# A planner's rules and costs in a causal convolution with a top-2 mixture of experts: idle slots filled, GpSimd and waits costed anew, row scatters spread further, margin of filled rows 2.2 instead of 3.0

## The chip, the cores and the metric

The kernel runs on one core of one Trainium2 chip. The time is in device microseconds for one execution; lower is better. Engines are named as in the profile: PE (matmul), PEld (weight load), DVE (vector), ACT (scalar), POOL (GpSimd) and SP (sync, here an issuer of DMAs).

## The reference

```python
# 1. causal depthwise convolution, 7 taps, softmax weights per head (8 heads of 24 columns)
w = softmax(weight, axis=-1)                       # 8 x 7
out[b, s, h, :] = sum_k w[h, k] * x_pad[b, s + k, h, :]
x = out.reshape(28672, 192)
# 2. top-2 of 8 experts, 192 -> 1024 -> 192
noisy = x @ w_gate + log1p(exp(x @ w_noise)) * noise
top2  = indices of the two largest of noisy;  g = softmax over those two
for e in range(8):
    y[rows of e] += g[rows of e] * (relu(x[rows of e] @ w1[e]) @ w2[e])
```

## The kernel before, in words

**Tiling.** The 28,672 tokens are worked in 28 units of 1,024 (`U`, `TU` = 8 tokens on each of 128 partitions). A unit is loaded (`xt`), convolved (PE for the first three units, then DVE lines L560 and L562), scaled, split into two fp16 parts (`rb`, two buffers), and its gate logits are formed on PE (L637). DVE then runs the routing chain (L658 to L702), PE counts ranks (L709 for units 0 to 4, L721 and L723 later, fed by `sums` of L719), DVE turns ranks into row numbers (L726 to L747), and POOL scatters the unit's rows to the region of each expert in DRAM: 16 indirect DMAs of 128 rows of 800 bytes each (L768), two for each of the 8 tokens of a partition.

**Blocks.** An expert's region is read in rounds, the first of 128 rows, then 28 of 256. A block is one round of one expert, 232 in all. SP loads it transposed (`bT`, L908 and L911, three buffers), PE runs 40 matmuls into `ph` (L848, two halves of 20), ACT and DVE evacuate each half into `h` as a high and a low part (L854, L858), PE runs 24 matmuls for each 128 rows into `py` (L866), ACT scales them into `y` (L872, six buffers) and POOL adds the rows to the output in DRAM with one indirect DMA for each 128 rows (L877). PE interleaves: the first product of block n, then the second of block n-1. At the start each expert's weights are split as well: `gram` on PE (L364), ACT the high part (L410), DVE the low part (L412).

**What sets the order.** Each engine executes its instructions in the order in which the program emits them. That order comes from a list scheduler in the kernel's own text: `Plan` keeps a clock for each engine and a set of threads (`conv`, `gating`, `scatters`, `run_blocks`, `results` and so on). A thread yields `(engine, cost)` before each piece, or a point in planned time, or a mark that another thread sets. `Plan.run` emits the piece with the smallest start minus urgency. No clock of the plan is in the built program: a cost there only moves an instruction to another place in its engine's order. Only semaphores hold an instruction back on the chip.

**Scatters and their pacing.** `scatters(u)` yields POOL 16 times with a pause of up to 2.0 planned us behind each, less when the unit's due time is near. Between two of them the plan may emit additions (L877).

**Rows that a round may read.** `ready_unit` says after how many units a round's rows are taken to be full: mean count less 3.0 sigma. A round's loads wait on the scatters of the units up to that one, and `lmin` pushes a later unit's rows behind any round already open to reading. An expert with more than 7,296 rows would run extra blocks in a loop at the end. For these inputs the eight experts get 7,067 to 7,242 rows; no unit is pushed by `lmin`, with 3.0 or with 2.2, and no extra block runs.

Of the kernel before, what the change touches and what calls it, by code (L numbers as in the profile page):

```python
# [19 lines left out]
TU = 8  # L20
# [25 lines left out]
class Plan:  # L46
# [5 lines left out]


    GAP = 0.1

    def __init__(self, **clock):
        self.clock, self.threads, self.now = clock, [], 0.0
# [32 lines left out]
    def run(self):  # L90
        self.spawned = []
        while True:
            best = None
            for th in self.threads:
                if th[1] is None:
                    continue
                eng = th[1][0]
                at = max(self.clock[eng], th[0] + (self.GAP if th[4] != eng else 0.0))
                if len(th[1]) > 2:
                    free = th[1][2].ready()  # L100
                    if free is None:
                        continue
                    at = max(at, free)
                urge = th[3](at) if callable(th[3]) else th[3]
                if best is None or at - urge < best[0]:
                    best = at - urge, at, th
            if best is None:
                assert not self.threads, "threads wait for each other"
                return
            _, at, th = best  # L110
            op = th[1]
            if len(op) > 2:
                op[2].taken += 1
            self.now = th[0] = self.clock[op[0]] = at + op[1]
            th[4] = op[0]
            self.step(th)
            while self.spawned:
                self.step(self.spawned.pop())
# [6 lines left out]
def kernel(  # L125
# [25 lines left out]
    mean = P * TU * 2 // E  # L151
# [4 lines left out]

    def ready_unit(end):
        for u in range(U):
            if mean * (u + 1) - 3.0 * sigma * math.sqrt(u + 1) >= end:
                return u  # L160
        return U - 1

# [100 lines left out]
    def done(*key, after=0.0):  # L263
        plan.mark(mark(*key), after)
# [329 lines left out]
    def gating():  # L594
        for u in range(U):
# [9 lines left out]
            if u < NTR:  # L605
                for t in range(0, 3 * TU, 8):
                    yield PE, 0.6, py_ring
                    if xT is None:
                        xT = small.tile([P, TU, 3, P], F16, name="xT", bufs=1)
                    pt = psum.tile([P, 512], F32, name="py", bufs=2)  # L610
                    pt = pt.bitcast(F16).rearrange("p (t n) -> p t n", n=P)
                    for i in range(8):
                        nc.tensor.transpose(pt[:, i], rb[:, (t + i) // 3, (t + i) % 3 * P:((t + i) % 3 + 1) * P], ident16)  # L613
                    yield ACT, 1.05
                    nc.scalar.activation(xT.rearrange("p t c n -> p (t c) n")[:, t:t + 8, :], pt, AF.Copy)
                    plan.freed(py_ring)
            else:
                for t in range(TU):
                    yield SP, 1.27
                    if xT is None:  # L620
                        xT = small.tile([P, TU, 3, P], F16, name="xT", bufs=1)
                    nc.sync.dma_start(xT[:, t], rb[:, t, 0:384], transpose=True)  # L622
                yield plan.now + 2.5
            if u == 0:
                yield mark("gates")
            yield PE, 1.1 if u < NTR else 0.7
# [80 lines left out]
            if u < NTR:  # L707
                yield PE, 0.45
                nc.tensor.matmul(rk[:, :TU * E], before, M.rearrange("p t e -> p (t e)"), start=True, stop=False,  # L709
                                 skip_group_check=True)  # L710
                for t in range(TU):
                    nc.tensor.matmul(rk[:, (t + 1) * E:W], ones16,
                                     M[:, t, None, :].to_broadcast([P, TU - t, E]),
                                     start=False, stop=(t == TU - 1), skip_group_check=True)
            else:
                yield DVE, 0.7
                sums = small.tile([P, TU + 1, E], F16, name="sums")
                with nc.allow_low_precision("counts of at most eight"):
                    V.tensor_reduce(sums, windows(Ms[u % 2]), axis=AX.X, op=OP.add)  # L719
                yield PE, 0.1  # L720
                nc.tensor.matmul(rk[:, :W], ones16, sums.rearrange("p t e -> p (t e)"), start=True, stop=False,  # L721
                                 skip_group_check=True)
                nc.tensor.matmul(rk[:, :TU * E], before, M.rearrange("p t e -> p (t e)"), start=False, stop=True,  # L723
                                 skip_group_check=True)
# [34 lines left out]
    def scatters(u, rbf, idx):  # L759
        if u:  # L760
            yield mark("scattered", u - 1)
        if reach[u + 1] > lo_row:
            yield mark("zero rows")
        for i in range(2 * TU):
            t, k = i // 2, i % 2
            yield POOL, 1.05
            apart()
            s = nc.gpsimd.indirect_dma_start(  # L768
                out=xsf, out_offset=bass.IndirectOffsetOnAxis(ap=idx[:, k, t:t + 1], axis=0),
                in_=rbf[:, t, :], in_offset=None)  # L770
            for v in scat:
                tc.declare_no_dep(s.ins, group=f"scat{v}", reason="every routed row has its own place")
            tc.declare_no_dep(s.ins, group="loads", reason="rows behind those of the blocks done")
            scat[u].append(s)
            tc.add_to_no_dep_group(f"scat{u}", s.ins)
            if reach[u + 1] > lo_row:
                for z in init:
                    needs(s, z)
            slack = (due(u) - 40.0 - plan.now) / (2 * TU - i)
            if u > 1:  # L780
                yield plan.now + min(2.0, max(0.0, slack - 1.0))
        done("scattered", u, after=2.5)

    def load_meta(j):
# [129 lines left out]
            done("block", n, after=2.3)  # L914

    def round_meta(j, mt):
        yield plan.now + 2.3
        if j:
            yield mark("first", (j - 1) * E + E - 3)
            yield mark("scale", E - 1)  # L920
        yield DVE, 1.9
        s, T = rounds[j]
        metas[j] = meta(mt, T // P, runs[:, ready[j] + 1, :], float(s))
        if j:
            unscale(metas[j][1], slice(0, E), T // P)
        done("meta", j)
        if j == 0:
            for e in range(E):
                yield mark("scale", e)
                yield DVE, 0.2  # L930
                unscale(metas[0][1][:, e:e + 1, :], slice(e, e + 1), T // P)
                done("gate", e)
# [9 lines left out]
    def results(n, half, py, adds):  # L942
# [7 lines left out]
        plan.freed(py_ring)  # L950
        if n:
            yield mark("added", n - 1)
        yield POOL, 1.6
        add_rows(j, ids[:, e, half:half + 1], y, adds)
        plan.freed(y_ring, 2.0)
        if half == rounds[j][1] // P - 1:
            done("added", n, after=2.5)

    def second(n):
        j, e = blocks[n]  # L960
# [105 lines left out]
```

## Time and profile before

| | |
|---|---|
| median of 3 runs | 2117.39 us (2103.3, 2117.39, 2119.4) |
| the profiled execution | 2097.99 us, its span 2096.2 us |
| busy share of the span | PE 95%, PEld 85%, DVE 75%, POOL 61%, ACT 38% |
| blocks | 232, 9,280 first and 10,944 second matmuls |

The page gives busy time by engine, the span in 40 slices, the DMA queues, the chain that ended last and the costliest groups of instructions. Behind it stand views of the trace: busy time in chosen stretches, waits (who waited for whom), and the instructions of an engine in order of time. "issue" in a wait means that the engine waited for nothing that the profile shows.

### The profile page before, as it was taken

To read this page: it belongs to the slowest core of one execution; us is meant where nothing else is said; L and a number is where in the kernel's file an instruction comes from. 1 tells how busy PE (TensorE), PEld (TensorE's weight loads), DVE (VectorE), ACT (ScalarE), POOL (GpSimd) and SP (SyncE) were. 2 spreads that over 40 slices of the span, in tenths; PEclk is the share of its full clock that TensorE was granted. 3 is DMA by queue.
4 is the path that set the end of the run, shared out by engine and by line. 5 is a ranking of instruction groups with operands and counts; after the bars stand their busy time and mean duration, and the time that the engine had idled before them with its cause. 6 is when DMAs were issued, how large, how long until landed. Compare 5 with 4: busy or idle time off the path is not lost.

```text
span 2096.2 us, 52494 instructions
## 1 busy us (share of the span) xinstructions
PE 1983.7 (95%) x21703; PEld 1778.0 (85%) x21703; DVE 1565.0 (75%) x4042; ACT 803.3 (38%) x1173; POOL 1271.8 (61%) x915
## 2 busy tenths in 40 slices
PE   7557999999999999999999999999999999999997
PEld 6546888878888899889899998988898888999986
DVE  6677888878888898889988888889899753333232
ACT  4334343333334343443343434433443433333332
POOL 0353576765666776777667777777767665333333
PEclk9778999999999999999999999999999999999999
DMA  8733456876657677666777766677777664444442
GB/s 238 196 91 79 86 98 118 155 148 118 117 92 125 130 132 128 122 126 117 118 129 133 126 130 117 113 120 131 130 132 115 107 98 77 58 61 57 60 58 35
DMA packets 521882, 236.99 MB, mean 113 GB/s; under 512 B 401304, under 2 KB 508824, under 8 KB 521505
## 3 DMA queue, kind: packets, MB, share of 16 engines
q1 hardware_dynamic: 433824, 142.72, 33.2%
q0 software_dynamic: 87200, 90.80, 29.3%
q8 instruction: 171, 2.80, 0.6%
q14 instruction: 79, 0.65, 0.1%
q10 hardware_dynamic: 608, 0.02, 0.0%
HBM read 40.12 MB, written 115.38 MB: 74 GB/s over the span
## 4 chain that ended last, share of the span: by engine, by line
PE 88%; DVE 5%; issue 3%; SPq 2%; ACT 1%; DMA 1%; another core or an unknown queue 0%; ACTq 0%; POOL 0%; DVEq 0%; POOLq 0%
PE ph L848 43%; PE py L866 41%; PE ph L514 1%; SPq L622 1%; PE misc L637 1%; DVE h L858 1%; PE grams L364 1%; DVE xc L562 0%; DMA xT<-rb 0%; DVE w1s L412 0%; SPq L911 0%; DVE w2s L412 0%; PE py L613 0%; DVE t L673 0%
## 5 line engine op out<-in xcount | busy, mean ns | idle before, releaser
L877 POOL DMA_INDIRECT out_dram<-y,ids x456 | 776.0, 1702 | 593.2 <-ACT y L872 423.5
L848 PE MATMUL ph<-bT,w1s 128*128 128x256 f16 (+2 forms) x9280 | 1004.7, 273 | 26.6 <-issue 10.3
L866 PE MATMUL py<-w2s,h 128*128 128x192 f16 x10944 | 953.1, 246 | 12.0 <-issue 11.3
L848 PEld LDWEIGHTS <-w1s 128*128 128x128 f16 (+1 forms) x9280 | 773.2, 98 | 210.6 <-issue 116.6
L866 PEld LDWEIGHTS <-h 128*128 128x128 f16 x10944 | 910.0, 98 | 23.8 <-issue 18.3
L858 DVE SCALAR_TENSOR_TENSOR h<-ph,h 128x1024 f16<-128x1024 f32 (+1 forms) x464 | 557.5, 1203 | 389.8 <-ACT h L854 345.2
L854 ACT ACTIVATE h<-ph 128x1024 f16<-128x1024 f32 (+1 forms) x464 | 468.0, 1009 | 556.8 <-PE ph L848 469.1
L768 POOL DMA_INDIRECT xs<-rb,idx x448 | 494.2, 1103 | 212.7 <-issue 144.7
L562 DVE SCALAR_TENSOR_TENSOR xc<-xt,wt,xc 128x192 f32<-128x192 f32 x1224 | 422.9, 410 | 3.3 <-DMA xt<-zero 3.3
L872 ACT ACTIVATE y<-py,ga 128x192 f32<-128x192 f32 x456 | 191.5, 421 | 602.2 <-PE py L866 439.2
L514 PE MATMUL ph<-xt,dg 128*128 128x192 f32 x280 | 50.8, 339 | 14.9 <-DMA xt<-in_x_dram 11.6
L514 PEld LDWEIGHTS ph<-xt,dg 128*128 128x128 f32 x280 | 47.3, 197 | 15.3 <-DVE dg L494 11.5
L560 DVE TENSOR_SCALAR xc<-xt,wt 128x192 f32<-128x192 f32 x204 | 53.9, 330 | 1.2 <-DMA xt<-in_x_dram 0.5
L575 DVE TENSOR_REDUCE am<-xc 128x8 f32<-128x1536 f32 x28 | 49.0, 1752 | 4.4 <-ACT xc L569 3.7
L579 DVE TENSOR_TENSOR xc<-xc,xs 128x1536 f32<-128x1536 f32 x28 | 49.3, 1761 | 0.0
L637 PE MATMUL misc<-gparts,xT 128*128 128x32 f16 (+1 forms) x752 | 27.4, 175 | 16.7 <-issue 15.3
L673 DVE SCALAR_TENSOR_TENSOR t<-t,t 128x64 f32<-128x64 f32 x168 | 38.1, 227 | 5.7
L637 PEld LDWEIGHTS <-xT 128*128 128x128 f16 x752 | 24.4, 97 | 19.8 <-issue 17.6
L589 DVE TENSOR_TENSOR rb<-xc,rb 128x1024 f16<-128x1024 f32 x28 | 34.1, 1217 | 4.3 <-ACT rb L585 2.1
L585 ACT ACTIVATE rb<-xc 128x1024 f16<-128x1024 f32 x28 | 29.5, 1053 | 11.1 <-DVE xc L579 9.3
L483 ACT ACTIVATE xt<-xt 128x1152 f32<-128x1152 f32 x27 | 31.2, 1156 | 0.0
L719 DVE TENSOR_REDUCE sums<-M 128x72 f16<-128x576 f16 x23 | 27.0, 1172 | 0.0
(142 smaller groups left out, 620.0 us busy)
## 6 DMA issues: line engine op xcount, KB each, us to landing
out_dram<-zero SPq DMA_DIRECT2D x28, 768.0 KB
xt<-in_x_dram SPq DMA_DIRECT2D x27, 768.0 KB
bT<-xs SPq DMA_TRANSPOSE x464
out_dram<-y,ids POOLq DMA_INDIRECT x456
xs<-rb,idx POOLq DMA_INDIRECT x448
w2s<-in_moe_w_dram SPq DMA_DIRECT2D x16, 384.0 KB
w1s<-in_moe_w_dram SPq DMA_DIRECT2D x8, 512.0 KB
w1s<-in_moe_w_dram SPq DMA_DIRECT2D x16, 256.0 KB
```

What stands on the lines that cost most here:

```text
L514: nc.tensor.matmul(c[:, h - h0, :TU * G].rearrange("p (t g) -> p t g", g=G), diag[h, k], xts[u][:, k:k + TU, h * G:(h + 1) * G], start=(k ...
L560: V.tensor_scalar(dst, src, wt[:, h, k:k + 1], None, op0=OP.mult)
L562: V.scalar_tensor_tensor(dst, src, wt[:, h, k:k + 1], dst, op0=OP.mult, op1=OP.add)
L579: V.tensor_tensor(xc, xc, xsc[:, :, None].to_broadcast([P, TU, D]), op=OP.mult)
L637: nc.tensor.matmul(lg[:, t], xT[:, t, c, :], g[:, gc], start=(i == 0), stop=(i == len(seq) - 1))
L768: s = nc.gpsimd.indirect_dma_start(out=xsf, out_offset=bass.IndirectOffsetOnAxis(ap=idx[:, k, t:t + 1], axis=0), in_=rbf[:, t, :], in_offs ...
L848: nc.tensor.matmul(ph[:, f, :T], w, x, start=f // 2 not in banks[:i], stop=f // 2 not in banks[i + 1:], skip_group_check=True)
L854: nc.scalar.activation(h[:, 0, half * nf:(half + 1) * nf, :T], ph[:, :, :T], AF.Relu)
L858: V.scalar_tensor_tensor(h[:, 1, hs, :T], ph[:, :, :T], 0.0, h[:, 0, hs, :T], op0=OP.max, op1=OP.subtract)
L866: nc.tensor.matmul(py[:, :D], h[:, a, f, ts], w2_part(e, lo, f), start=(n == 0), stop=(n == 3 * FC - 1))
L872: nc.scalar.activation(y, py[:, :D], AF.Copy, scale=gate)
L877: a = nc.gpsimd.indirect_dma_start(out=out, out_offset=bass.IndirectOffsetOnAxis(ap=ids, axis=0), in_=y, in_offset=None, compute_op=OP.add)
```

## The change

Six edits, all in the planner's rules and in the costs that threads yield:

- `Plan.run` collects every thread that could go (`able`). When the chosen piece would start late, another piece for the same engine that would end before that start goes first.
- A piece that follows one on PE in the same thread starts 0.3 later in the plan (`DRAIN`).
- Planned costs: a scatter 1.4 (was 1.05), an addition 2.0 (1.6), `sums` 1.1 (0.7) and 1.0 more before its matmul, the transposed rows of the logits 5.0 (2.5), a round's row data 4.0 (2.3), an added block 2.8 behind (2.5).
- The pause behind a scatter goes up to 2.6 (was 2.0).
- `ready_unit` takes 2.2 sigma (3.0). Rounds 9 to 16 then count as full one unit earlier; all others stand as before.

```diff
+    DRAIN = 0.3
...
-            best = None
+            best, able = None, []
...
-                at = max(self.clock[eng], th[0] + (self.GAP if th[4] != eng else 0.0))
+                gap = 0.0 if th[4] == eng else self.GAP + (self.DRAIN if th[4] == "PE" else 0.0)
+                at = max(self.clock[eng], th[0] + gap)
...
+                able.append((at - urge, at, th))
                 if best is None or at - urge < best[0]:
-                    best = at - urge, at, th
+                    best = able[-1]
...
+            for one in able:
+                if one[2][1][0] == best[2][1][0] and one[1] + one[2][1][1] <= best[1]:
+                    if one[0] < best[0] or one[1] < best[1]:
+                        best = one
...
-            if mean * (u + 1) - 3.0 * sigma * math.sqrt(u + 1) >= end:
+            if mean * (u + 1) - 2.2 * sigma * math.sqrt(u + 1) >= end:
...
-                yield plan.now + 2.5
+                yield plan.now + 5.0
...
-                yield DVE, 0.7
+                yield DVE, 1.1
...
+                yield plan.now + 1.0
                 yield PE, 0.1
...
-            yield POOL, 1.05
+            yield POOL, 1.4
...
-            slack = (due(u) - 40.0 - plan.now) / (2 * TU - i)
+            slack = (due(u) - 45.0 - plan.now) / (2 * TU - i)
             if u > 1:
-                yield plan.now + min(2.0, max(0.0, slack - 1.0))
+                yield plan.now + min(2.6, max(0.0, slack - 1.4))
...
-        yield plan.now + 2.3
+        yield plan.now + 4.0
...
-        yield POOL, 1.6
+        yield POOL, 2.0
...
-            done("added", n, after=2.5)
+            done("added", n, after=2.8)
```

No instruction is added or removed on PE, DVE, ACT or SP; the order moves. Line numbers of the changed kernel are 7 or 8 higher from the margin on (L768 becomes L776, L877 becomes L885, L858 becomes L866).

**POOL, unit 6.** The order on POOL around the scatters (L768) of unit 6, with the additions (L877, two for a block of 256 rows) between them. Before:

```order
L768 DMA xs<-rb_190,idx 287744x200 x5
L877 DMA out_dram<-y,ids 28928x192 x2
L768 DMA xs<-rb_190,idx 287744x200 x5
L877 DMA out_dram<-y,ids 28928x192 x2
L768 DMA xs<-rb_190,idx 287744x200 x4
L877 DMA out_dram<-y,ids 28928x192 x2
L768 DMA xs<-rb_190,idx 287744x200 x2
```

And now:

```order
L776 DMA xs<-rb_190,idx 287744x200 x2
L885 DMA out_dram<-y,ids 28928x192 x2
L776 DMA xs<-rb_190,idx 287744x200 x3
L885 DMA out_dram<-y,ids 28928x192 x2
L776 DMA xs<-rb_190,idx 287744x200 x3
L885 DMA out_dram<-y,ids 28928x192 x2
L776 DMA xs<-rb_190,idx 287744x200 x3
L885 DMA out_dram<-y,ids 28928x192 x2
L776 DMA xs<-rb_190,idx 287744x200 x2
L885 DMA out_dram<-y,ids 28928x192
L776 DMA xs<-rb_190,idx 287744x200
L885 DMA out_dram<-y,ids 28928x192
```

Five scatters to a block became three, and the last two (not shown) stand behind the tenth addition. Additions between the first and the last scatter of a unit, before and now: unit 2: 1, 2; unit 3: 7, 8; units 4 to 8: 6 each, now 10, 8, 10, 10, 8; unit 9: 8, 8; unit 10: 9, 8; unit 11: 10, 11; unit 12: 10, 12; units 13 to 27: 12 to 13, now 12 to 14.

**DVE, behind the routing of unit 1.** `h` are the low parts of the first blocks, `w1s` and `w2s` low parts of weights, `rb` the rows of unit 2. Before:

```order
L579 TENSOR_TENSOR xc<-xc,xs 128x1536
L858 SCALAR_TENSOR_TENSOR h<-ph,h 128x4x128 x2
L412 SCALAR_TENSOR_TENSOR w1s_131<-w1s_132,ws,w1s_131 128x1024
L589 TENSOR_TENSOR rb_190<-xc,rb_190 128x8x128
L591 TENSOR_TENSOR rb_190<-xc,rb_190 128x8x64
L858 SCALAR_TENSOR_TENSOR h<-ph,h 128x4x128 x2
```

And now, where behind `w1s_131` (which follows `xc`) ten small instructions of the first round's row data come first:

```order
L824 TENSOR_TENSOR ga<-ga,mt 128x8
L825 TENSOR_TENSOR ga<-ga,gb 128x8
L596 TENSOR_TENSOR rb_190<-xc,rb_190 128x8x128
L598 TENSOR_TENSOR rb_190<-xc,rb_190 128x8x64
L866 SCALAR_TENSOR_TENSOR h<-ph,h 128x4x128 x2
```

The first block's low parts moved behind a weight split, ten small instructions and the two of `rb`.

**ACT, from the first blocks to unit 2's routing.** `t` is the exponential inside unit 2's routing chain, `h` the high parts, `xT` the transposed rows for unit 2's logits. Before:

```order
L615 ACTIVATE xT<-py 128x1024 x2
L872 ACTIVATE y<-py,ga 128x192
L615 ACTIVATE xT<-py 128x1024
L483 ACTIVATE xt<-xt 128x1152
L854 ACTIVATE h<-ph 128x4x128
L662 ACTIVATE t_1419<-t_1419 128x64
L854 ACTIVATE h<-ph 128x4x128
L872 ACTIVATE y<-py,ga 128x192
L704 ACTIVATE d<-d 128x8
```

And now:

```order
L622 ACTIVATE xT<-py 128x1024
L490 ACTIVATE xt<-xt 128x1152
L622 ACTIVATE xT<-py 128x1024
L862 ACTIVATE h<-ph 128x4x128
L622 ACTIVATE xT<-py 128x1024
L862 ACTIVATE h<-ph 128x4x128
L417 ACTIVATE w1s_132<-w1s_133,ws 128x1024
L417 ACTIVATE w2s_149<-w2s_150,ws 128x768
L669 ACTIVATE t_1486<-t_1486 128x64
```

On PE, likewise, the first product of block 2 now stands ahead of unit 2's logits and not between logits and ranks, and the weight split of the expert after it moved ahead of the exponential.

## Rows read from the trace of the kernel before

**Rows 1.** The page: the span, and the instruction queue (packets, MB, share).

```profile
span 2096.2 us, 52494 instructions
...
q8 instruction: 171, 2.80, 0.6%
```

**Rows 2.** Busy time by stretch: us, then per engine busy (xinstructions), PEclk, DMA share, GB/s.

```profile
97.00:200.00 103.00, 65.11 (x729) 55.98 (x727) 76.62 (x221) 39.05 (x53) 46.29 (x39) 0.75 0.30 70
200.00:2083.00 1883.00, 1856.35 (x20467) 1662.78 (x20465) 1426.55 (x3602) 725.08 (x1048) 1204.37 (x848) 1.00 0.64 110
```

**Rows 3.** Waits of PE over the span: us in total, times, longest us.

```profile
PE misc L709 <- DVE M L702: 17.3, 2, 11.7
PE misc L637 <- issue: 15.3, 22, 1.2
...
PE py L866 <- issue: 11.3, 25, 1.2
PE ph L848 <- issue: 10.3, 25, 1.2
PE ph L848 <- DVE w1s L412: 7.4, 4, 3.3
...
PE grams L364 <- issue: 5.7, 8, 1.1
...
PE misc L721 <- DVE sums L719: 2.2, 3, 1.3
```

**Rows 4.** Busy time from first to last scatter of units 4 to 11 and 14.

```profile
298.50:333.10 34.60, 31.70 (x321) 27.48 (x319) 26.78 (x61) 12.27 (x17) 28.16 (x22) 0.96 0.69 139
369.90:407.60 37.70, 36.03 (x402) 31.94 (x401) 32.09 (x74) 15.22 (x21) 30.61 (x22) 1.00 0.82 155
433.40:467.80 34.40, 30.21 (x286) 24.38 (x284) 26.21 (x65) 10.73 (x15) 27.99 (x22) 0.90 0.78 158
496.20:535.10 38.90, 36.01 (x383) 31.86 (x381) 32.29 (x73) 15.20 (x21) 30.69 (x22) 1.00 0.73 150
560.50:594.40 33.90, 30.55 (x303) 26.11 (x302) 26.06 (x55) 11.28 (x16) 27.50 (x22) 0.95 0.76 165
622.00:663.60 41.60, 41.07 (x463) 36.79 (x461) 37.73 (x82) 17.04 (x26) 32.97 (x24) 1.00 0.76 149
683.80:726.50 42.70, 41.25 (x455) 35.94 (x452) 35.97 (x83) 15.35 (x23) 32.90 (x25) 1.00 0.72 146
743.10:791.20 48.10, 48.10 (x544) 43.51 (x542) 43.96 (x109) 20.07 (x29) 38.23 (x26) 1.00 0.76 139
...
924.40:976.90 52.50, 52.45 (x592) 47.63 (x590) 47.38 (x118) 21.73 (x33) 38.90 (x28) 1.00 0.70 131
```

**Rows 5.** POOL in time: start, us, what [idle before <-releaser]; units 6, 14.

```profile
444.99 1.07 POOL L768 DMA_INDIRECT xs<-rb,idx  x1 [0.30 <-issue]
...
928.11 1.74 POOL L877 DMA_INDIRECT out_dram<-y,ids  x1 [1.47 <-ACT y L872]
```

**Rows 6.** SP in time: zeros written to the output in units 6 and 11.

```profile
442.43 0.58 SPq L433 DMA_DIRECT2D out_dram<-zero  x1
...
763.28 0.43 SPq L433 DMA_DIRECT2D out_dram<-zero  x1
```

**Rows 7.** DVE in time, behind the routing of unit 1 and in that of unit 2.

```profile
103.34 1.28 DVE L412 SCALAR_TENSOR_TENSOR w1s<-w1s,ws,w1s 128x1024 f16<-128x1024 f32 x1
...
106.28 1.28 DVE L858 SCALAR_TENSOR_TENSOR h<-ph,h 128x512 f16<-128x512 f32 x2
...
130.12 0.16 DVE L389 TENSOR_SCALAR wf<-misc 128x4 int32<-128x4 int32 x1 [0.99 <-PE misc L247]
...
132.90 0.69 DVE L858 SCALAR_TENSOR_TENSOR h<-ph,h 128x512 f16<-128x512 f32 x1 [0.93 <-ACT h L854]
...
143.35 1.28 DVE L412 SCALAR_TENSOR_TENSOR w1s<-w1s,ws,w1s 128x1024 f16<-128x1024 f32 x1
```

**Rows 8.** PE in time: half of block 2's first product.

```profile
127.37 2.20 PE L848 MATMUL ph<-bT,w1s 128*128 128x128 f16 x20
```

## The prediction, made before the changed kernel was run

> **What bounds the kernel.** I read the page first, then busy time by stretch, then PE's waits, then the same two views again around the scatters of single units, and last the engines in order of time. The span is 2096.2 us [rows 1]. From 200 to 2083 us PE is busy for 1856.4 of 1883.0 us at the full clock [rows 2]; every microsecond that PE loses there moves the end, and nothing else does. From 97 to 200 us PE is busy for only 65.1 of 103 us, at a mean granted clock of 0.75 (a mix of the levels 1.2 and 2.4 GHz), while DVE is busy for 76.6 [rows 2]. So there are two places to gain: that opening, and the 27 us idle later on.
>
> The reader should then look at what ended PE's idle time [rows 3]. The four rows with "issue" sum to 15.3 + 11.3 + 10.3 + 5.7 = 42.6 us: PE stood still although no tile, no semaphore and no buffer was late. They are many short gaps of up to 1.2 us (80 in all). What the wait is for is my reading, not a row: instructions reach the engines by DMA, 171 packets of together 2.80 MB on a queue of their own [rows 1], so a matmul can be late because its instruction is.
>
> **When it happens** is in [rows 4], one row for each unit from its first scatter to its last. Undisturbed PE starts 592 matmuls in 52.5 us (unit 14) or 544 in 48.1 (unit 11), 11.3 a microsecond. By that rate units 4 to 8 should have done their matmuls in 28.4, 35.6, 25.3, 33.9 and 26.8 us; they took 34.6, 37.7, 34.4, 38.9 and 33.9. The loss is 6.2 + 2.1 + 9.1 + 5.0 + 7.1 = 29.5 us, slow matmuls at the lower clock included (the clock column reads 0.90 in unit 6). Unit 9, in 41.6 us, lost 0.6; unit 10, in 42.7, lost 2.4; units 11 and 14 nothing. The difference is how close the 16 scatters stand. In units 4 to 8 there are six additions between first and last scatter, five scatters to a block. A scatter takes about 1.07 us behind a gap of 0.30, an addition 1.74 [rows 5], so five and two cost 5 x 1.37 + 2 x 2.04 = 10.9 us on POOL against 8.1 us for a block (88 matmuls and its share of 26 for a unit's logits and ranks, 91 at 11.3 a microsecond): POOL issues without pause, [0.30 <-issue]. In unit 14 it waits for `y`, and so runs at PE's pace [rows 5].
>
> **The change, part by part.**
>
> *Scatters of units 3 to 11.* Three scatters and two additions cost 3 x 1.37 + 2 x 2.04 = 8.2 us, about a block. Units 4, 6 and 7 get ten additions between first and last, as unit 11 had: loss 0 by that row. Units 5 and 8 get eight, as unit 9 had: 0.6 each. Unit 10 goes from nine to eight. The upper bound of the gain is therefore 29.5 - 1.2 = 28.3, say 29 us; the lower is 0, if spacing has nothing to do with it. Unit 10, with more additions than unit 9, lost more, so the count does not settle it alone. I charge each of units 4 to 8 with unit 10's 2.4 us: 29.5 - 12 = 17.5, taken as **18 us gained**.
>
> *Unit 2.* Its scatters stood as nine, one addition, seven; now five, one, five, one, six. PE's starvation in that stretch is the larger part of the 5.7 us on L364 [rows 3] and a little on L866. I take 3 us gained, bounds 0 and 5.7.
>
> *The first blocks.* `h` of the first block ran 2.9 us behind the weight split that followed it closely before (103.34 to 106.28 is that split and the two of `rb` [rows 7]); now these and ten small instructions at 0.16 us or a little more, about 1.3 us, come first: block 1 starts 4.2 us later. Block 2's first product moves ahead of the logits: 2 x 2.20 = 4.4 us [rows 8]. Against that, unit 2's chain loses the waits of 0.99 and 0.93 and two low parts of 0.69 [rows 7], and gains one split of 1.28: 1.9 + 1.4 - 1.3 = 2.0 us shorter, with three tiny rows besides. PE stood idle for 17.3 - 11.7 = 5.6 us for this chain [rows 3]. If instructions arrive no faster than before up to the logits, PE does the moved work while it would have starved, and the ranks come about 2 us earlier; if not, up to 3 us later (4.2 + 4.4 less the 5.6 idle before). I take 0. Behind the ranks, block 3 waited for a split that began only at 143.35 [rows 7], with 3.3 us as the longest such wait [rows 3]; that split now stands inside the chain. I take 3 us gained, bounds 0 and 5. The opening together: 0 + 3 + 3, **6 us gained**, bounds 11 gained and 6 lost (3 for the ranks, 3 more if the longer idle time drops the clock as it did around the waits of this stretch, mean 0.75 [rows 2]).
>
> *Later waits for logits and ranks.* The added 2.5 and 1.0 in the plan move PE's instructions behind more blocks. L721's 2.2 us [rows 3] go: **2 us gained**, bounds 2 gained and 1 lost.
>
> *The rest is free.* The margin moves the loads of rounds 9 to 16 to one unit less; PE shows no wait on a block load in [rows 3], so there is nothing to shorten, and no unit is pushed in either version. Later scatters in units 13 to 27 end some blocks later but stay ahead of their round. An x load now issued one block sooner stands in SP's queue ahead of a block's load; three buffers hide that, and it would cost only if SP waited longer than a block.
>
> **Sum.** 18 + 6 + 2 = 26 us against the profiled 2097.99: 2072. That execution was below all three timed ones; their median is 19.4 us higher. I subtract from the median: 2117.4 - 26 = **2091 us**.
>
> A rule speaks against this. The Trainium skill, Runtime: NRT & Kernel Launch, section Instruction fetch mechanics, says that instructions are streamed in 16 KiB blocks during execution and that the cost of crossing one is "mostly hidden". The trace agrees on the size (2.80 MB in 171 packets) and not on the cover: 42.6 us of issue gaps. By the rule spacing would give nothing, and the time would be that of the first rival.
>
> **The rivals.**
>
> 1. *Not the spacing.* The starved stretches also hold the zero write of 768 KB and the x load. In unit 6 the zero write was issued at 442.43 [rows 6], within its window. If such transfers starve PE, whatever the scatters do, only 6 + 2 us are left: 2109. For: each dense window holds one. Against: the zero write of unit 11's stretch was issued at 763.28 [rows 6], within 743.1 to 791.2, and cost nothing [rows 4].
> 2. *The opening loses.* The low parts come 4.2 us late, the clock stays down and the ranks slip: 6 lost, while the spacing gives half, 9. With 2 for the later waits: 2117 + 6 - 9 - 2 = 2112.
> 3. *Slower.* Units 13 to 27 now scatter over up to 14 additions of the 16 of a round. If the pause between two units' scatters is what lets instructions catch up, its shrinking starves every unit. At unit 10's 2.4 us, 16 units from 12 to 27 lose 38 us: 2117 + 38 - 8 = 2147. It decides once units from 13 on show issue gaps of 1 us each or more. Against it: wider has always meant less in [rows 4].
> 4. *The plan does not reach the chip.* POOL's pace is set by `y` and by its own instructions, not by the plan's clock, and bunches of three may starve PE as well as five do. Then 2117.
>
> **How the numbers follow.** My forecast gets 0.55, rival 1 0.20, rival 2 0.10, rival 3 0.08, rival 4 0.07. The bounds are 2117 - 29 - 11 - 2 = 2075 and, from the profiled execution's level 19 us lower, some way below that; the upper side takes in rivals 1, 2 and 4. Range **2066 to 2119**; it leaves out rival 3 and the ends of the others. Within 1% (21 us) a measurement of this kernel can't tell a change from none: the four executions shown here differ by that much. Faster by over 1% is below 2096. The forecast at 2091 is only 5 us beyond, with bounds wide on both sides: 0.8 of its 0.55, and little of rivals 1 and 2, make 0.49. Slower takes rival 3, 0.08. The rest, 0.43, is within 1%.
>
> **What would show it.** In the profile after: windows from first to last scatter of units 4 to 8 over 40 us wide with 11 matmuls a microsecond; the four issue rows of PE at 25 us or less in sum, nearly all of it before 170 us; PE busy for over 1850 us between 200 us and its last matmul, with that matmul 20 us or more sooner; the ranks of unit 2 at their old time, give or take 3 us, and the first block of 256 rows some 6 us sooner. Wrong would be: wide windows with the same gaps (rivals 1, 4), gaps in units 13 and later (rival 3), or a wait of PE for `h` or a block load that was not there.

## The result, and the profile after

| | before | after |
|---|---|---|
| first comparison, 4 runs each | 2114.63 us median (2103.3 to 2119.4) | 2089.97 us median (2087.42 to 2096.86) |
| ratio | | 0.9896, interval 0.9849 to 0.9944 |
| last comparison, 14 and 7 runs | 2097.11 us median | 2082.01 us median, ratio 0.991 (0.9876 to 0.9944) |
| a comparison on another chip, 28 and 12 runs | 2040.71 us median | 2045.3 us median, ratio 1.0013 (0.998 to 1.0046) |

The change saves about 1%: 24.7 us by the medians of the first comparison, 15.1 by the larger last one. On another chip, where the kernel before is 74 us faster, it saves nothing. Below, the chip of the last comparison is called A (its profiles look like those of the first) and the other B.

The two profiled executions of the first comparison differ by less than the medians, 2097.99 and 2087.42 us: that of the kernel before was faster than all four timed ones. Of these 10.6 us, 6.4 are won before PE's first block of 256 rows (it started at 198.45, now at 192.09), the rest behind it.

**Span and stretches.** From the page, then busy time by stretch (columns as in [rows 2]), profile after:

```profile
span 2085.6 us, 52483 instructions
...
q8 instruction: 171, 2.80, 0.6%
```

```profile
97.00:200.00 103.00, 69.56 (x785) 59.55 (x783) 84.29 (x241) 43.48 (x59) 47.74 (x40) 0.76 0.34 81
200.00:2073.00 1873.00, 1848.23 (x20403) 1655.12 (x20400) 1412.79 (x3580) 718.83 (x1043) 1198.94 (x847) 1.00 0.65 110
```

PE is busy 4.5 us more in the opening than in [rows 2]. Behind it, 26.6 us of idle time became 24.8: hardly less.

**Waits of PE** after, the same view as [rows 3]:

```profile
PE ph L856 <- issue: 17.9, 41, 1.0
PE misc L716 <- DVE M L709: 15.8, 2, 9.5
PE misc L644 <- issue: 11.8, 14, 1.9
...
PE py L874 <- issue: 8.0, 22, 1.1
PE ph L856 <- ACT w1s L417: 6.6, 3, 4.9
PE ph L856 <- DVE h L866: 6.5, 2, 6.2
```

The issue rows sum to 37.7 us against 42.6. The 2.2 us on `sums` are gone. The wait of 6.2 us for `h` (1.6 before) is for the low parts of the first block, which the change put behind ten small instructions.

The issue rows again, behind 200 us alone, before and after:

```profile
PE ph L848 <- issue: 10.3, 25, 1.2
PE py L866 <- issue: 9.7, 23, 1.2
PE misc L637 <- issue: 1.0, 3, 0.6
```

```profile
PE ph L856 <- issue: 12.9, 30, 1.0
PE py L874 <- issue: 7.3, 20, 1.1
PE misc L644 <- issue: 1.4, 3, 0.5
```

They sum to 21.0 us before and 21.6 after. Behind the opening the starvation (PE's idle time that the profile puts down to "issue") did not become less in this profile; it moved.

**Around the scatters** after, busy time from first to last scatter of units 4, 5, 6, 7, 8, 9, 10, 11 and 14, the view of [rows 4]:

```profile
291.30:341.90 50.60, 49.84 (x556) 44.66 (x555) 44.10 (x106) 19.80 (x29) 41.01 (x26) 1.00 0.76 133
368.10:420.50 52.40, 49.44 (x538) 42.69 (x535) 43.37 (x122) 16.02 (x26) 29.30 (x24) 1.00 0.84 170
432.40:475.90 43.50, 42.29 (x469) 37.41 (x467) 37.16 (x108) 14.66 (x23) 34.00 (x26) 1.00 0.86 130
486.90:531.30 44.40, 43.09 (x482) 38.29 (x479) 38.71 (x99) 16.11 (x24) 36.77 (x26) 1.00 0.70 129
549.30:595.70 46.40, 45.60 (x513) 41.10 (x511) 42.05 (x112) 17.79 (x26) 37.50 (x24) 1.00 0.68 118
615.80:653.70 37.90, 35.34 (x389) 30.72 (x387) 29.90 (x72) 11.70 (x18) 30.86 (x24) 1.00 0.76 136
682.40:724.70 42.30, 39.20 (x409) 32.98 (x407) 33.62 (x90) 13.41 (x21) 32.89 (x24) 0.96 0.61 104
736.50:785.40 48.90, 46.34 (x512) 40.81 (x510) 42.11 (x105) 18.01 (x26) 37.45 (x27) 1.00 0.67 117
917.30:978.30 61.00, 61.00 (x685) 55.23 (x683) 55.52 (x144) 25.46 (x37) 42.58 (x30) 1.00 0.71 125
```

By 11.3 matmuls a microsecond, units 4 to 8 now lose 1.4, 4.8, 2.0, 1.7 and 1.0, together 10.9 us; in [rows 4] they lost 29.5. That is 18.6 us won. But units 9, 10 and 11 lose 3.5, 6.1 and 3.6, where they lost 0.6, 2.4 and nothing: 10.2 us given back. Unit 9's window became narrower (37.9 from 41.6 us), unit 10's stayed as it was (42.3 from 42.7), unit 11's too (48.9 from 48.1). Unit 12, not shown, loses 2.4 more than before. Unit 14 loses 0.4.

These counts differ between executions of one order. In `after_third`, the changed kernel once more, units 4 to 8 lose 11.9 us and units 9 to 11 lose 3.4, 2.6 and 2.5.

### The profile page after: what moved, and what is told of

Same layout as the page of the kernel before. It is cut to its first block, busy times and chain, and to the rows that moved or that the text cites. A ratio compares the mean times of both kernels' runs of the same rounds, so it can differ in the third digit from the quotient of the medians.

```text
span 2085.6 us, 52483 instructions
## 1 busy us (share of the span) xinstructions
PE 1980.8 (95%) x21703; PEld 1774.8 (85%) x21703; DVE 1559.3 (75%) x4042; ACT 801.1 (38%) x1173; POOL 1267.9 (61%) x915
## 4 chain that ended last, share of the span: by engine, by line
PE 91%; DVE 3%; issue 2%; another core or an unknown queue 1%; SPq 1%; ACT 1%; DMA 0%; ACTq 0%; POOL 0%; DVEq 0%; POOLq 0%
PE ph L856 45%; PE py L874 42%; PE ph L521 2%; PE misc L644 1%; SPq L629 1%; PE grams L371 0%; DVE xc L569 0%; DVE h L866 0%; DVE w1s L419 0%; PE py L620 0%; DVE xc L567 0%; ACT h L862 0%; DMA xt<-zero 0%; DVE dg L501 0%
## 5 line engine op out<-in xcount | busy, mean ns | idle before, releaser
L885 POOL DMA_INDIRECT out_dram<-y,ids x456 | 798.5, 1751 | 572.5 <-ACT y L880 415.7
L866 DVE SCALAR_TENSOR_TENSOR h<-ph,h 128x1024 f16<-128x1024 f32 (+1 forms) x464 | 557.9, 1203 | 339.3 <-ACT h L862 307.0
L776 POOL DMA_INDIRECT xs<-rb,idx x448 | 467.8, 1044 | 226.5 <-issue 138.1
L644 PE MATMUL misc<-gparts,xT 128*128 128x32 f16 (+1 forms) x752 | 26.0, 175 | 12.9 <-issue 11.8
L592 ACT ACTIVATE rb<-xc 128x1024 f16<-128x1024 f32 x28 | 29.5, 1054 | 21.5 <-DVE xc L586 17.3
L419 DVE SCALAR_TENSOR_TENSOR w1s<-w1s,ws,w1s 128x1024 f16<-128x1024 f32 x16 | 20.5, 1282 | 11.1 <-ACT w1s L417 5.6
```

Source lines behind the costliest of these rows:

```text
L644: nc.tensor.matmul(lg[:, t], xT[:, t, c, :], g[:, gc], start=(i == 0), stop=(i == len(seq) - 1))
L776: s = nc.gpsimd.indirect_dma_start(out=xsf, out_offset=bass.IndirectOffsetOnAxis(ap=idx[:, k, t:t + 1], axis=0), in_=rbf[:, t, :], in_offs ...
L866: V.scalar_tensor_tensor(h[:, 1, hs, :T], ph[:, :, :T], 0.0, h[:, 0, hs, :T], op0=OP.max, op1=OP.subtract)
L885: a = nc.gpsimd.indirect_dma_start(out=out, out_offset=bass.IndirectOffsetOnAxis(ap=ids, axis=0), in_=y, in_offset=None, compute_op=OP.add)
```

## The experiments

Three groups of four kernels, each compared with the kernel before on its own chip: the first two groups on B, the last on A. Ratios are to the kernel before. On A the kernel before was not profiled; where a profile from A is set against one of before, that one is from the first comparison. Blocks are counted from 0, and times of a block are the start of its first product on PE.

### 1. The POOL numbers alone, and all the rest alone (chip B)

`pool_only` is the kernel before with

```diff
-            yield POOL, 1.05
+            yield POOL, 1.4
-            slack = (due(u) - 40.0 - plan.now) / (2 * TU - i)
+            slack = (due(u) - 45.0 - plan.now) / (2 * TU - i)
-                yield plan.now + min(2.0, max(0.0, slack - 1.0))
+                yield plan.now + min(2.6, max(0.0, slack - 1.4))
-        yield POOL, 1.6
+        yield POOL, 2.0
-            done("added", n, after=2.5)
+            done("added", n, after=2.8)
```

and `all_but_pool` is the changed kernel with these five lines as before.

> Only the edits on POOL (scatter 1.4, pause up to 2.6, slack 45, addition 2.0 and 2.8) on the kernel before; rules of the scheduler, margin and other costs as before. Theory S (the spacing of scatters carries the gain, the rest is small): 10 to 20 us faster than before, ratio 0.990 to 0.995, and fewer issue gaps of PE from 240 to 860 us than the 20 us of before. Theory R (the scheduler's rule and the other costs carry it, by the opening): within 5 us of before. Units 4 to 8 get 8 to 10 additions between first and last scatter here, unit 9 ten (eight in the changed kernel), so S also expects less starvation in unit 9 than the changed kernel has.

> The changed kernel with the five POOL numbers put back (1.05, 2.0, 40, 1.6, 2.5), so six additions stand in units 4 to 9 again. Theory S: the gain shrinks to that of the opening, 5 to 8 us (ratio 0.996 to 0.998), and PE's issue gaps from 240 to 860 us are 20 us or more. Theory R: 20 to 25 us faster, as the whole change.

Measured: the kernel before 2039.01 us, `pool_only` 2028.61 (0.9954, 0.9937 to 0.9972), `all_but_pool` 2076.29 (1.0185, 1.0153 to 1.0216). So on B the POOL numbers win 10 us without any starvation to remove, and the other edits without them lose 37.

These five numbers do not move the scatters alone. The plan reorders the other engines with them: in `pool_only`, as in the changed kernel, the first product of block 2 stands ahead of unit 2's logits. Its first block of 256 rows starts at 164.96 us, that of the kernel before on this chip at 169.31, and 4.3 of the 6.9 us between the two profiles are won there. So this pair does not part the spacing from the opening, as theories S and R had it.

Where the other edits lose: SP, POOL and PE in time or by wait, `all_but_pool`:

```profile
384.12 14.42 SPq L452 DMA_DIRECT2D xs<-zero  x8
...
394.23 0.99 POOL L776 DMA_INDIRECT xs<-rb,idx  x1 [7.70 <-DMA xs<-zero]
...
402.25 0.99 POOL L776 DMA_INDIRECT xs<-rb,idx  x1 [7.03 <-DMA xs<-zero]
...
PE ph L856 <- DMA bT<-xs: 19.5, 2, 13.5
...
PE py L874 <- ACT y L880: 12.9, 10, 2.3
PE ph L856 <- DVE h L866: 12.4, 8, 4.5
```

Eight writes of zero rows (L452) stand in a row on SP's queue. They wait for scatters, the scatters behind them wait for these writes, and block loads stand behind both: PE waits up to 13.5 us for `bT`. Before, the writes went out as four and four with a block load between. From block 32 to block 40, around these writes, `all_but_pool` takes 15.8 us more than the profile of the kernel before on B; in all its profile is 49.3 us behind at the last block. The rest arises later, up to block 88 at 884 us, where PE's waits for `y` and `h` lie.

### 2. Wider still, and dense in the late units (chip B)

`wide_07` gives every unit from 3 on a fixed pause, `dense_late` removes the pause from unit 13 on and halves the planned cost of a scatter there:

```diff
-                yield plan.now + min(2.6, max(0.0, slack - 1.4))
+                yield plan.now + (0.7 if u > 2 else min(2.6, max(0.0, slack - 1.4)))
```

```diff
-            yield POOL, 1.4
+            yield POOL, 0.7 if u >= 13 else 1.4
-            if u > 1:
+            if 1 < u < 13:
```

> The changed kernel with a fixed planned pause of 0.7 behind each scatter from unit 3 on, whatever the slack: 12 to 14 additions between first and last scatter in all units but 18 and 19 (8 and 10). Theory S, refined by the trace of the changed kernel (starvation comes where POOL issues for 20 us and more without waiting for y, as in units 7 and 9 to 11): the 16 us of issue gaps and the slow matmuls with them between 240 and 860 us go, 15 to 25 us below the changed kernel, about 2070. Theory T (time or transfers set it: the gaps end at about 860 us in both kernels whatever the scatters do): the gaps before 860 us stay and the time is within 5 us of the changed kernel.

> The changed kernel with units 13 to 27 scattered densely: no pause and a planned cost of 0.7, so that four to six additions stand between first and last scatter instead of 12 to 14; nothing else is edited. Theory S: issue gaps appear in 860 to 1750 us, where the changed kernel has 1.6 us, 3 to 6 us a unit and as much again in slow matmuls: 60 to 130 us slower. Theory T: no gaps there and within 10 us of the changed kernel.

Measured: `wide_07` 2055.63 us (1.0084, 1.0066 to 1.0102), `dense_late`, two executions, 2124.29 (1.0416, 1.039 to 1.0442). In `dense_late` PE's issue gaps are 0, and yet it is the slowest on this chip. What ended waits of ACT, then of PE, in `dense_late`:

```profile
ACT y L880 <- DMA out_dram<-y,ids: 550.1, 206, 12.6
...
PE py L874 <- ACT y L880: 42.9, 27, 5.4
PE ph L856 <- DVE h L866: 20.9, 14, 6.0
```

Dense scatters hold up the additions behind them on POOL, the six buffers of `y` fill, ACT stands in front of them, and PE stands behind ACT. That cost of density was in no part of the prediction. Theories S and T differ by starvation alone, and B has none, so neither run decides between them. PE and SP by wait, `wide_07`:

```profile
PE ph L856 <- DMA bT<-xs: 22.7, 2, 16.4
...
SPq L289 <- DVE xc L569: 82.7, 21, 24.7
SPq L796 <- DMA xs<-rb,idx: 82.6, 25, 9.2
```

Scatters that end late hold a round's loads on SP, by up to 9.2 us (L796). But the longest wait of PE, 16.4 us for `bT`, has another wait of SP ahead of it: SP stood 24.7 us in front of an x load (L289) until DVE's convolution was through. It lies in unit 18. At block 128 `wide_07` is 0.3 us behind the profile of the kernel before on B, at block 144 it is 22.1 behind, and it ends 21.1 behind. In that stretch lie units 18 and 19, the two that its plan scatters over 8 and 10 additions. Units 7 to 17, with 14 additions each, lose 0.3 to 0.7 us by the count of 11.3 a microsecond. So these runs show a cost of density, and a cost where the plan with the wide pause closes up again; that wide spacing costs by itself is not shown.

### 3. Both kernels again, the fill rule, the margin (chip B)

`before_again` and `after_again` are the two kernels unaltered; `no_fill` is the changed kernel without the loop that fills holes; `margin_30` has the margin as before:

```diff
-            for one in able:
-                if one[2][1][0] == best[2][1][0] and one[1] + one[2][1][1] <= best[1]:
-                    if one[0] < best[0] or one[1] < best[1]:
-                        best = one
```

```diff
-            if mean * (u + 1) - 2.2 * sigma * math.sqrt(u + 1) >= end:
+            if mean * (u + 1) - 3.0 * sigma * math.sqrt(u + 1) >= end:
```

> The kernel before unedited, for its profile on the same chip as after_again. If the chip does not starve PE: fewer than 2 us of issue gaps, the first block of 256 rows near 170 us instead of 195.7, and the rest of the difference to the first profile between 200 and 860 us. If it starves: issue gaps of about 40 us, as in the first profile.

> The changed kernel unedited, beside the kernel before on one chip. In the last four runs the chip showed nearly no issue gaps of PE (0.5 us in all against 42.6 in the profile of before) and the kernel before took 2039 us. Theory S': the gain of the change is the starvation that it takes away and so needs a chip or a state that starves; where PE is not starved, the change is worth -5 to +5 us. Theory O: the order itself (opening, waits) is worth its 10 us or so everywhere: ratio 0.99 to 0.996 in either state. Theory H: the scheduler's rule loses where starvation does not hide it, as the changed kernel with the POOL numbers put back did (37 us slower than before): ratio over 1.005.

> The changed kernel without the scheduler's new rule (the loop over able that puts a piece into an idle slot); DRAIN, margin and all costs stay. Theory H (the rule loses): 10 us and more faster than the changed kernel, near the kernel with the POOL edits alone (0.995 of before). Otherwise within 5 us of the changed kernel.

> The changed kernel with the margin of 3.0 sigma again: rounds 9 to 16 wait for one unit more; the planned order of POOL is the same but for one place in unit 11. My prediction called the margin free: within 3 us of the changed kernel. The other way (the block loads of rounds 9 to 16 then come late, since scatters end later than before): PE waits for bT at the head of rounds 9 to 12, 5 to 20 us slower.

Measured: before 2040.71 us; `before_again`, one execution, 2034.45; `after_again` 2045.3 (1.0013); `no_fill` 2024.97 (0.995, 0.9926 to 0.9974); `margin_30` 2042.94 (1.002, 0.9989 to 1.0051). The margin is free. The fill rule loses 20.3 us on B, more than the 15.7 that the rest of the change wins there.

**No starvation on B.** Issue waits of ACT and DVE in the kernel before, on the chip of the first comparison:

```profile
ACT y L872 <- issue: 73.9, 55, 3.1
...
DVE h L858 <- issue: 40.4, 38, 4.8
```

and the same two rows in `before_again`, with its windows of units 4 and 8, as dense as in [rows 4]:

```profile
ACT y L872 <- issue: 8.6, 7, 1.6
...
DVE h L858 <- issue: 1.7, 2, 1.3
```

```profile
268.60:303.20 34.60, 34.60 (x381) 31.46 (x379) 33.24 (x77) 14.51 (x21) 28.17 (x22) 1.00 0.87 162
...
519.40:554.00 34.60, 34.60 (x394) 31.12 (x393) 32.19 (x95) 12.12 (x19) 28.11 (x22) 1.00 0.78 142
```

PE is busy for the whole of each window, and has no issue row at all. So close scatters do not starve PE by themselves. Where PE starves, ACT and DVE show issue waits as well, in all parts of the run. That the chip decides whether there is starvation, and close scatters only where PE pays for it, fits these rows and is not shown. One stretch speaks against reading too much into a single profile: unit 0 scatters without a pause (64 to 85 us) in the same order in both kernels named here, and beside it PE's logits of unit 1 wait 8.5 us in ten issue gaps in the first profile of the kernel before, 0.4 us in one gap in `pool_again` on A.

**Where the fill rule loses on B.** POOL, ACT and PE in time in `after_again`, with ACT's waits over the span:

```profile
376.67 0.99 POOL L776 DMA_INDIRECT xs<-rb,idx  x1 [8.29 <-DMA xs<-zero]
383.57 0.99 POOL L776 DMA_INDIRECT xs<-rb,idx  x1 [5.92 <-DMA xs<-zero]
...
695.57 1.06 ACT L592 ACTIVATE rb<-xc 128x1024 f16<-128x1024 f32 x1 [9.49 <-DMA xs<-rb,idx]
757.03 1.06 ACT L592 ACTIVATE rb<-xc 128x1024 f16<-128x1024 f32 x1 [8.95 <-DMA xs<-rb,idx]
...
760.31 3.90 PE L856 MATMUL ph<-bT,w1s 64*128 64x256 f16 x20 [5.26 <-DVE h L866]
...
ACT y L880 <- DMA out_dram<-y,ids: 120.6, 63, 5.5
ACT rb L592 <- DMA xs<-rb,idx: 33.6, 9, 9.5
```

and ACT's waits in `no_fill`:

```profile
ACT y L876 <- DMA out_dram<-y,ids: 6.7, 7, 1.0
```

POOL loses 14.2 us to the zero rows, and since three scatters and two additions take it as long as a block, it does not catch up: from 390 to 740 us ACT waits for buffers of `y` again and again. Then ACT, which runs in order, stands 9 us in front of `rb` until the scatters of two units earlier are through; `h` stands behind it, and PE waits 5.3 us. From block 64 to block 88 (631 to 849 us), where three such waits lie (the third is 8.15 us, at 820.70) with slow matmuls behind each, `after_again` takes 20.9 us longer than `no_fill`. In `no_fill` POOL lost 6.9 and 4.9 us to the zero rows, written as six and two, and no backlog came of it. Nor did one in the changed kernel's profile of the first comparison, although POOL lost 8.19 and 5.98 us there to the same eight writes: ACT waited 8.8 us in all for buffers of `y`, against 120.6 here. So the time lost to the zero rows is not enough to explain it. What tips POOL over is not shown by these runs, and `after_again` itself took 2026 to 2031 us in 3 of its 12 runs and 2041 to 2052 in the others.

### 4. The zero rows moved, the POOL numbers and the changed kernel again (chip A)

`zeros_apart` gives the zero rows out as four and four, `zeros_u4` two units earlier; PE's and POOL's orders stay those of the changed kernel. `pool_again` and `after_third` are `pool_only` and the changed kernel once more.

```diff
-        for e in range(E):
-            yield SP, 0.5
-            init.append(nc.sync.dma_start(
+        for e in [0, 1, 2, 3, None, 4, 5, 6, 7]:
+            yield (SP, 0.5) if e is not None else plan.now + 6.0
+            if e is not None: init.append(nc.sync.dma_start(
```

```diff
-            if u == 6:
+            if u == 4:
                 plan.spawn(zero_rows())
```

> The changed kernel with one thing put back as before: the eight writes of zero rows behind the regions of the experts go out as four and four, around one more block load, and not eight in a row. PE's and POOL's orders are the same as in the changed kernel, word for word. Theory A (on the second chip the lost 20 us of the changed kernel begin there: POOL waits 8.3 and 5.9 us for these writes, stays two blocks behind because three scatters and two additions take it as long as a block, ACT then waits for buffers of y 120 us in sum, and at last stands 8 to 9 us in front of rb): ratio to before 0.995 at most, about 2025 us where before takes 2040, ACT's waits for y's buffers under 20 us. Rival B (POOL is too close to its limit whatever sets it back; the zero writes are only one occasion): ratio 1.000 to 1.003 and y's waits again around 100 us. On a chip where before takes 2110 us: A no difference from the changed kernel beyond 5 us, since six and two already stood apart there.

> The changed kernel with the eight writes of zero rows given out two units earlier, when no scatter needs them yet; PE's and POOL's orders are the same as in the changed kernel. Theory A: POOL's waits for xs<-zero go (14 us to under 3), and the time is as of the four-and-four version or up to 5 us better, about 2020 to 2025 on the chip where before takes 2040. Rival B: 2040 to 2046. A third way: SP holds its block loads for scatters in flight in the same way two units earlier, PE waits for bT, and nothing is won.

> The kernel before with only the five POOL numbers of the change (scatter 1.4, addition 2.0, pause 2.6, due 45, added 2.8), once more. On the chip where before takes 2040: 0.995 again, 2027 to 2033. On a chip where before takes 2110 and PE shows 40 us of issue gaps: the theory of the prediction says these numbers alone carry the 18 us (ratio 0.991 or less), the rival that spacing is not it says 0.997 or more.

> The changed kernel unaltered, as the measure for the others of this call. On the chip where before takes 2040: ratio 1.001, runs of two kinds, some at 2026 to 2031 and most at 2041 to 2051. On a chip where before takes 2110: ratio 0.990, 2090.

Measured: before 2097.11 us; `zeros_apart` 2079.21 (0.9904, 0.9867 to 0.9942), `zeros_u4` 2079.87 (0.9907, 0.9877 to 0.9938), `pool_again` 2072.72 (0.988, 0.9842 to 0.9919), `after_third` 2082.01 (0.991). The zero rows make no difference on A. Theory A and rival B of the expectations (letters that have nothing to do with the two chips) give different times only on chip B, so that part is inconclusive: what sets POOL back there stays open. The reason given for no difference on A was wrong: six and two is the order of `no_fill`, and the changed kernel writes eight in a row on both chips.

The POOL numbers alone, with all that they reorder, carry all of the gain on A. Windows of units 7, 9, 10 and 11 in `pool_again`, then its issue waits:

```profile
475.20:517.90 42.70, 38.88 (x406) 32.71 (x404) 32.87 (x87) 14.45 (x22) 35.38 (x25) 0.96 0.72 142
...
596.60:641.60 45.00, 44.56 (x498) 39.90 (x496) 41.14 (x102) 17.96 (x27) 37.38 (x26) 1.00 0.75 146
654.30:699.90 45.60, 45.23 (x508) 40.68 (x506) 39.90 (x91) 18.16 (x27) 36.05 (x26) 1.00 0.75 140
712.10:763.90 51.80, 51.31 (x573) 46.18 (x572) 45.09 (x111) 21.04 (x30) 37.90 (x28) 1.00 0.74 133
```

```profile
PE misc L637 <- issue: 7.6, 10, 1.3
PE ph L848 <- issue: 7.2, 17, 1.0
...
PE py L866 <- issue: 5.2, 12, 1.0
...
PE grams L364 <- issue: 1.0, 3, 0.4
```

Units 9 to 11 lose 0.9, 0.6 and 1.1 us here against 3.5, 6.1 and 3.6 in the changed kernel's first profile, and the issue gaps are 21.0 us in sum. But units 4 to 8 lose 3.9, 0.7, 4.6, 6.8 and 0.5, together 16.5 us, against 10.9. From the first block of 256 rows to the last block it took 1863.6 us, before 1872.6. In the opening it is 19.6 us ahead of the profile before, and 12.0 ahead of `after_third` on the same chip; so about two thirds of its lead over before is opening, not spacing. 6.1 of the 19.6 are there when the first block starts (91.00 against 97.06 us), ahead of the first scatter that the edit moved, so not all of that can be its doing.

## Why the prediction was right

**The number.** 2091 us was forecast, 2089.97 measured, 1 us apart. Most of that closeness is luck. The sum of 26 us was taken off the median of the kernel before, and the medians differ by 24.7 us; but the two profiles, in which the terms can be read, differ by 10.6, and the larger comparison by 15.1. Of its terms 18 + 6 + 2 the first was mis-sized, the second came out in sum, and of the third only its row is seen to be gone.

**The opening, 6 us: held in sum.** The first block of 256 rows came 6.4 us sooner (7.6 in `after_third`). Unit 2's ranks stand at 140.34 us, 139.97 before, as the 0 said. Block 1's product starts 4.2 us later (107.10 against 102.87 us), which is the 4.2 of the prediction. Block 3's wait of 3.3 us for its split is gone, but block 5 now waits 4.9 us for the high part of its own (3.0 before), which I had not priced. PE's issue gaps at the `grams` and at unit 2's logits are gone; others of up to 1.04 us stand in the first products of blocks 2 and 4 instead. `pool_again` came 12.0 us further than `after_third` in the same stretch, so the other edits may cost more in the opening than they win; one profile of each does not settle it.

**The later waits, 2 us.** The row on `sums` is gone from PE's waits. That the end moved by it is not shown.

**The scatters, 18 us: mis-sized.** In units 4 to 8 they gave 18.6 us, by the prediction's own count. What failed is the step that took the starvation of a unit for gone once its scatters stand further apart, and so priced units 9 to 11 at nothing because they had eight or more additions already ("Unit 10 goes from nine to eight", "0.6 each"). They lost 10.2 us more than before, so the term measured 8.4 us by these windows, and 6.0 with unit 12. PE's issue gaps behind 200 us were 21.0 us before and 21.6 after. From the first block of 256 rows to the last one the change took 4.4 us off. `after_third`, `zeros_apart` and `zeros_u4`, with the same orders on PE, DVE, ACT and POOL, took off 8.2, 0.1 and 12.9 us in that stretch: one profile shows a term of this size only roughly.

Why units 9 to 11 lost more is open. The count of additions does not order the losses: unit 9 kept its eight and lost 2.9 us more. Neither does the width of the window: unit 5 has the widest of units 4 to 8, 52.4 us, and loses the most of them, and "wider has always meant less" was not so in [rows 4] either (unit 10 lost more than unit 9, unit 7 more than unit 5). Nor is it enough that POOL, at 8.2 us for three scatters and two additions against a block's 8.1, issues without waiting: in unit 9 of `pool_again` it is busy for 37.38 of 45.0 us, and 25 gaps of 0.30 fill the rest, yet PE loses 0.9. The nearest test of the spacing on a chip that starves is `pool_again`, and that moves the opening too; dense scatters in the changed kernel were not run there. So that spacing carries what was won behind the opening is argued, not shown.

**What was named as evidence.** Units 4 to 8 are over 40 us wide: right, but at 10.3 to 11.1 matmuls a microsecond instead of 11. Four issue rows of 25 us or less, nearly all before 170 us: wrong, 37.7 us, of which 21.6 behind 200. PE busy for over 1850 us behind 200: 1848.2, just missed. PE's last matmul 20 us sooner: 10.75 us in the two profiles. No gaps in units 13 and later: right, 1.6 us in all behind 860 us; rival 3 was right that starvation moves, and had the wrong units.

**The reading of the issue gaps.** The prediction read them as instructions that reach PE late by DMA. ACT and DVE show such waits on the chips where PE does, and hardly any on B, so the cause is not PE's alone. But the trace's DMA packets do not bear the reading out. In the kernel before no instruction packet was under way between 109.9 and 127.9 us, and 12 of the 80 gaps, 7.9 of the 42.6 us, lie between 116.1 and 126.9. An instruction packet took 0.92 us on average there, and as long on B. What the waits are for stays open. The Trainium skill, Runtime: NRT & Kernel Launch, section Instruction fetch mechanics, calls the cost of crossing an instruction block "mostly hidden". On B the trace agrees (no issue row of PE in `before_again`, with the same 171 packets); since the gaps of the first comparison are not shown to be such crossings, they do not contradict it.

**The rest was free: held for the margin** (`margin_30`), not for the fill rule, which I had not costed as an edit of its own. On starving chips the profiles show no price for it behind the opening: from the first block of 256 rows to the last one the changed kernel took 1868.3 (first comparison) and 1864.4 us (A), `pool_again` 1863.6. But the same orders took 1872.5 in `zeros_apart` and 1859.8 in `zeros_u4`, so a price of some us would not show.

**What beats both.** `pool_again` on A (0.988) and `no_fill` on B (0.995) have lower medians than the changed kernel on the same chip. `no_fill` was not run on A. On B it leaves PE 0.2 us of waits behind 200 us.

## What to carry to other kernels

Before a wait is priced as removed, ask where it could go: check afterwards that it became less in sum, and not only in the places that the change aimed at (here 21.0 and 21.6 us). Profile one order more than once before a term of a few us is read from it. A cost in a planner moves the pieces of every engine, so compare all engines' orders before an experiment is said to test one thing alone. Look behind each in-order engine for the buffer that comes free last (here `y` and `rb`), because that is where a backlog reaches PE. And compare on more than one chip before a gain of 1% is put down to its mechanism.

## What was not expected of the hardware

- The same kernel takes 2041 us on chip B, 2097 on A and 2115 in the first comparison. Of 63.6 us between the two profiled spans, 29.1 arise before the first block of 256 rows (198.45 and 169.31 us), the rest behind it. Issue waits on three engines go with it; the cause is not shown.
- A chain of writes and scatters to one tensor in DRAM on two queues costs some 5 to 8 us for each change of queue: POOL waited 8.29 and 5.92 us, and 7.70 and 7.03 us, for zero rows (in `zeros_apart` 5.65, 4.81 and 4.76), and eight such writes took SP 14.42 us.
- PE's issue gaps are not bound to the landing of instruction packets (12 gaps with none under way), and beside the same sixteen close scatters of unit 0 they were 8.5 us in one profile and 0.4 in another.
